# Second-half score products that run on over columns behind the keys

## The chip, the cores and the metric

The kernel runs on one core of a Trainium2 chip. The metric is the device time of one execution in microseconds (us). Several runs of each kernel are made, and their median stands for the kernel.

## What is computed

Windowed attention with four sink keys over 4 batches, 8 heads, 768 positions and 64 dimensions a head, all in float32, and behind it a two-layer block with a leaky activation, on 3072 tokens of width 512 with 2048 hidden units.

```python
scores = scale * q @ k.T                      # scale = 1/8
keep = (pos_k < n_sink) | ((pos_q - pos_k >= 0) & (pos_q - pos_k < window))   # 4, 128
a = softmax(where(keep, scores, -1e9)); x = a @ v          # heads side by side: (3072, 512)
h = x @ w_in; g = max(h, 0) + alpha * min(h, 0); out = g @ w_out
```

## The kernel before

The 3072 tokens are cut into 12 chunks of 256 queries, each of which belongs to one batch. A chunk goes through attention, and its 16 blocks of 128 hidden units then go through the two layers. While the layers of chunk c run, the attention of chunk c + 1 is mixed in between, so that TensorE always has products to do. All operations are first described to a planner (class `Plan`), each with an assumed cost, and the planner writes out one fixed order for each engine. The order depends on the assumed costs and on nothing else.

**Score products** (function `unit`, lines 569 to 601). A unit is chunk c, head h and half u: 128 queries against 260 keys (128 of the block before, 4 sink keys, 128 of the query's own block). For chunks 2 to 11 it is two products that add up in one PSUM bank: line 597 with the high part of the queries as weights, line 598 with the low part, both over the same 260 columns of keys. In the first half (u = 0) of the chunks that open a batch (3, 6 and 9) there is no block before, and the products are 132 columns wide. Chunks 0 and 1 use another form (line 588).

Keys and queries of one head lie in one SBUF tile, `kq`, side by side: 392 columns of keys (`KC`), 256 of the queries' high part, 256 of their low part (`prep_head`, line 552). The second half reads the keys from column 132 to column 392, the end of the keys, so that what lies next in the tile is the queries' high part. There are two `kq` tiles, used in turn by the heads. The halves write into banks of the kind "s", of which there are two with 512 columns each, in turn.

**What reads the scores** (`soften`, line 603). VectorE adds the mask, keeps the row's extreme and writes to SBUF (line 610); it waits for the product of line 598, and when it is through, the bank is free for a later unit. ScalarE then takes the exponential (line 614). Later `finish_head` divides by the sums and the rest of attention follows.

**The layers.** `gemm1` does 12 products of 256 columns for each block of hidden units (line 894), ScalarE and VectorE make the activation (lines 898 to 901), and `gemm2` does six products of 512 columns (lines 931, 932 and 929). All products have a weight load of their own of 128 columns, which the profile lists apart (PEld).

In TensorE's order, a second-half pair stands mostly between the 12 products of line 894 and the six of `gemm2`; a first-half pair stands between `gemm2` and the next 12.

Of the kernel before, what the change touches and what calls it, by code (L numbers as in the profile page):

```python
# [22 lines left out]
NS = 4  # L23
WIN = 2 * P + NS
# [54 lines left out]
class Plan:  # L79
# [25 lines left out]
    def op(self, engine, cost, run, reads=(), writes=(), tail=0.09, mode=None, nbytes=0, other=None, locks=False):  # L105
        o = Op(engine, cost, tail, run, self.rank if engine == "PE" else None)
        o.ways = {engine: (cost, run)}
        if other:
            o.ways[other[0]] = other[1:]
        o.born = self.rank  # L110
        if engine == "PE":
            self.rank += 1
        o.mode, o.nbytes, o.index = mode, nbytes, len(self.ops)
        seen = []
        for group, writing in ((reads, False), (writes, True)):
            for x in group:
                v, key = x if isinstance(x, tuple) else (x, None)
                if v not in seen:
                    seen.append(v)
                keys = [k for k in set(v.wrote) | set(v.read) if key is None or k is None or k == key]  # L120
                for k in keys:
                    o.before.update(v.wrote.get(k, ()))
                    if writing:
                        o.before.update(v.read.get(k, ()))
                if writing:
                    for k in keys:
                        if key is None or k == key:
                            v.wrote.pop(k, None)
                            v.read.pop(k, None)
                    v.wrote.setdefault(key, []).append(o)  # L130
                else:
                    v.read.setdefault(key, []).append(o)
        for v in seen:
            v.left += 1
        o.values = seen
        o.takes = [v for v in seen if v.kind]
        o.locks = locks
        self.ops.append(o)
        return o
# [168 lines left out]
def mm(n):  # L308
    return 0.456e-3 * n


def native(n):
    return 1.667e-3 * n
# [8 lines left out]
def program(ctx, tc, qk, pairs, vp, vq, vs, w, par, out):  # L322
    nc = tc.nc
# [245 lines left out]
    def unit(c, h, u):  # L569
        if h == 0 and u == 0:  # L570
            nms[c], sink[c], sums[c] = val("nm"), val("sink"), val("sm")
            if c in SPLIT:
                s0 = sink[c]
                op("POOL", 0.15, lambda: nc.gpsimd.memset(s0.at, 0.0), writes=[s0])
        ko = u * (P + NS)
        qs = slice(u * P, (u + 1) * P)
        w0 = slice(0 if c % CPB or u else P, WIN)
        n = w0.stop - w0.start
        kw = slice(ko + w0.start, ko + WIN)
        if c in SPLIT:  # L580
            pair = (h, h + 1)
            banks_ = [val("s") for _ in pair]
            used = [prep[c, h][0]]

            def scores():
                for x, bk in zip(pair, banks_):
                    st, r = prep[c, x]
                    nc.tensor.matmul(bk.at[:, w0], st.at[r, :QC][:, qs], st.at[r, QC:][:, kw], start=True, stop=True)
            op("PE", 1.47 * native(n), scores, reads=used, writes=banks_, tail=N_TAIL, mode="row")
        else:  # L590
            pair = (h,)
            banks_ = [val("s")]
            kq, qh, ql, ks = prep[c, h]

            def scores():
                s = banks_[0].at
                nc.tensor.matmul(s[:, w0], qh()[:, qs], ks()[:, kw], start=True, stop=False)  # L597
                nc.tensor.matmul(s[:, w0], ql()[:, qs], ks()[:, kw], start=False, stop=True)  # L598
            op("PE", 2 * mm(n), scores, reads=[kq], writes=banks_, tail=R_TAIL)
        for x, bk in zip(pair, banks_):  # L600
            soften(c, x, u, bk)

    def soften(c, h, u, s):
        if u == 0:
            ptile_[c, h] = val("pt_")
        pt, nm, sm = ptile_[c, h], nms[c], sums[c]
        i = min((c % CPB) * 2 + u, 2)
        w0 = slice(0 if i else P, WIN)
        n = WIN if i else P + NS
        op("DVE", dve(n), lambda: nc.vector.tensor_tensor_reduce(  # L610
            out=pt.at[:, u, w0], in0=s.at[:, w0], in1=masks[:, i, w0], scale=-0.125, scalar=BIG,
            op0=ALU.add, op1=ALU.min, accum_out=nm.at[:, h, u:u + 1]),
            reads=[s, known("masks"), known(f"masks{i}")], writes=[(pt, u), (nm, (h, u))], tail=0.17)
        op("ACT", exp(n), lambda: nc.scalar.activation(  # L614
            pt.at[:, u, w0], pt.at[:, u, w0], AF.Exp, bias=nm.at[:, h, u:u + 1], scale=-1.0, accum_out=sm.at[:, h, u:u + 1]),
            reads=[(nm, (h, u))], writes=[(pt, u), (sm, (h, u))])
# [331 lines left out]
    def attention(c):  # L948
        def a_step(h, u):
            def run():  # L950
                if u == 0:
                    if h == 0 and c == PAIRED:
                        masks_in_order()
                    if h == 0 and c and c % CPB == 0:
                        vs_prep(c // CPB)
                    prep_head(c, h)
                    next_load()
                unit(c, h, u)
                if u == 1:
                    finish_head(c, h)  # L960
                    first = 1 if c >= PAIRED else 5
                    if h in range(first, first + (KT if c >= PAIRED else 2)):
                        load_v(c, h - first)
            return run
# [8 lines left out]
        if c in SPLIT:  # L973
            def pair_step(h, u):
                def run():
                    if u == 0:
                        for x in (h, h + 1):
                            prep_head(c, x)
                        for x in (h, h + 1):
                            next_load()  # L980
                    unit(c, h, u)
                    if u == 1:
                        for x in (h, h + 1):
                            finish_head(c, x)
                        if h in (0, 2) and c:
                            load_v(c, h // 2)
                return run
            steps = [pair_step(h, u) for h in range(0, H, 2) for u in range(2)]
            for at, st in ((8, lambda: av_split(c, 1)), (8, lambda: sk(1)), (5, lambda: av_split(c, 0)), (4, sk)):
                steps.insert(at, st)  # L990
            return steps
# [286 lines left out]
```

## Time and profile before

| | us |
|---|---|
| median of 3 runs | 677.34 |
| lowest, highest | 676.94, 677.88 |
| span of the profiled execution | 676.2 |
| TensorE busy, products | 663.8 |
| VectorE busy | 525.8 |
| ScalarE busy | 397.5 |

The span runs from the first instruction to the last in the profiled execution; the time of a run also holds what lies around it, so that the profiled execution stands 1.1 us under the median of the runs. Products overlap one another in TensorE's pipeline, and their listed durations are longer than the distance from one to the next; what a product costs in a stream is read from the chain of waits, which gives each only the time by which it moved the end.

### The profile page before, as it was taken

Reading aid. Unit: us, or ns where it says so; the run is one execution under the profiler, and the core shown is the slowest. Engines: PE = TensorE matmul, PEld = TensorE weight load, DVE = VectorE, ACT = ScalarE, POOL = GpSimd, SP = SyncE. Lnnn points to the kernel's source line nnn. Section 1 sums busy time; section 2 is a strip of 40 time slices with the busy share of each in tenths; the row PEclk is TensorE's granted clock in tenths of the full one; section 3 lists DMA queues with packets and bytes.
Section 4 is the critical chain, followed back from the end, with each engine's and each line's share of the span. In section 5 each row is a group of like instructions: output and inputs, shape, how many; then the busy total and the mean of one; then the engine's idle time right before and its main releaser. Section 6 shows DMA issues by size and latency. Waiting matters only on the chain.

```text
span 676.2 us, 13243 instructions
## 1 busy us (share of the span) xinstructions
PE 663.8 (98%) x4532; PEld 580.5 (86%) x4534; DVE 525.8 (78%) x1750; ACT 397.5 (59%) x1066; POOL 34.5 (5%) x115
## 2 busy tenths in 40 slices
PE   9989999999999999999999999999999999999996
PEld 4577898888989989989988988988998988998995
DVE  6999999968967976986986995995895994994331
ACT  6989888827636726736636735644744753853332
POOL 2110000001000000000000000010000000000000
PEclk9979999999999999999999999999999999999999
DMA  8684641424343453443443433552542543420001
GB/s 314 229 277 151 241 187 39 127 71 147 122 133 107 122 148 93 145 132 95 141 118 114 143 107 93 163 140 61 172 128 78 161 128 88 142 94 17 32 2 35
DMA packets 58683, 85.19 MB, mean 126 GB/s; under 512 B 9072, under 2 KB 35056, under 8 KB 58608
## 3 DMA queue, kind: packets, MB, share of 16 engines
q1 hardware_dynamic: 55056, 71.17, 34.7%
q10 hardware_dynamic: 3552, 13.11, 5.4%
q8 instruction: 37, 0.61, 0.4%
q14 instruction: 38, 0.31, 0.1%
HBM read 67.22 MB, written 17.04 MB: 125 GB/s over the span
## 4 chain that ended last, share of the span: by engine, by line
PE 83%; DVE 9%; ACT 5%; issue 2%; POOL 0%; DMA 0%; ACTq 0%; SPq 0%; POOLq 0%
PE bank L894 35%; PE bank L931 12%; PE bank L932 11%; PE bank L929 11%; PE bank L786 3%; PE bank L598 3%; PE bank L597 3%; PE bank L875 2%; DVE wa L396 2%; ACT pt L614 1%; ACT wa L382 1%; DVE wa L394 1%; DVE w L404 1%; DVE g L899 1%; DVE gl L901 1%
## 5 line engine op out<-in xcount | busy, mean ns | idle before, releaser
L894 PE MATMUL bank<-xh,w 128*128 128x256 f32 x1536 | 307.9, 283 | 0.4 <-DVE g L899 0.2
L894 PEld LDWEIGHTS bank<-xh,w 128*128 128x128 f32 x1536 | 250.6, 189 | 9.0 <-DVE g L899 3.0
L894 PE MATMUL bank<-xl,w 128*128 128x256 f32 x768 | 215.1, 280 | 0.1
L898 ACT ACTIVATE g<-bank,param 128x256 f32<-128x256 f32 x192 | 90.5, 472 | 117.4 <-PE bank L894 113.1
L931 PE MATMUL bank<-w,gh 128*128 128x512 f32 x382 | 151.7, 397 | 0.2 <-ACT gh L900 0.2
L932 PE MATMUL bank<-w,gh 128*128 128x512 f32 x382 | 150.1, 393 | 0.0
L894 PEld LDWEIGHTS bank<-xl,w 128*128 128x128 f32 x768 | 145.2, 189 | 4.4 <-DVE xl L808 0.3
L614 ACT ACTIVATE pt<-pt,nm 128x260 f32<-128x260 f32 (+1 forms) x192 | 94.5, 493 | 53.5 <-DVE nm L610 53.1
L899 DVE TENSOR_TENSOR g<-bank,g 128x256 f32<-128x256 f32 x192 | 79.7, 419 | 51.4 <-ACT g L898 50.9
L929 PE MATMUL bank<-w,gl 128*128 128x512 f32 x382 | 119.5, 394 | 0.0
L900 ACT CAST gh<-g 128x256 fp32r<-128x256 f32 x192 | 76.9, 404 | 59.7 <-DVE g L899 59.6
L901 DVE TENSOR_TENSOR gl<-g,gh 128x256 fp32r<-128x256 f32 x192 | 80.5, 423 | 26.5 <-ACT gh L900 23.0
L610 DVE CUSTOM_DVE_ANT_0 pt<-bank,masks 128x260 f32<-128x260 f32 (+1 forms) x192 | 75.0, 401 | 19.3 <-PE bank L598 15.5
L929 PEld LDWEIGHTS bank<-w,gl 128*128 128x128 f32 x382 | 70.7, 188 | 16.2 <-issue 0.7
L931 PEld LDWEIGHTS bank<-w,gh 128*128 128x128 f32 x382 | 71.9, 188 | 9.5 <-ACT gh L900 0.7
L932 PEld LDWEIGHTS bank<-w,gh 128*128 128x128 f32 x382 | 71.9, 188 | 8.3
L563 DVE TENSOR_TENSOR kq<-stage,kq 64x392 fp32r<-64x392 f32 x80 | 45.3, 566 | 2.7
L659 POOL TENSOR_TENSOR sink<-pt,ri 128x8 f32<-128x8 f32 x80 | 20.8, 264 | 504.7 <-DVE ri L644 358.8
L597 PE MATMUL bank<-kq 128*128 128x260 f32 (+1 forms) x160 | 44.4, 278 | 1.3 <-DVE nm L610 1.3
L598 PE MATMUL bank<-kq 128*128 128x260 f32 (+1 forms) x160 | 45.0, 281 | 0.0
L655 DVE CUSTOM_DVE_ANT_0 comb<-pt,ri 128x128 f32<-128x128 f32 x136 | 43.1, 343 | 0.4
L561 ACT CAST kq<-stage 128x392 fp32r<-128x392 f32 x80 | 40.9, 512 | 0.7 <-ACT pt L614 0.2
(130 smaller groups left out, 686.9 us busy)
## 6 DMA issues: line engine op xcount, KB each, us to landing
stage<-qk SPq DMA_DIRECT2D x80, 324.0 KB, 2.9
wraw<-w ACTq DMA_DIRECT2D x12, 1024.0 KB, 5.9
swap<-comb SPq DMA_DIRECT2D x36, 256.0 KB, 2.0
comb<-swap SPq DMA_DIRECT2D x36, 256.0 KB, 3.2
v<-vq SPq DMA_DIRECT2D x36, 192.0 KB, 2.5
out_dram<-ob SPq DMA_DIRECT2D x22, 256.0 KB, 3.5
wraw<-w SPq DMA_DIRECT2D x4, 1024.0 KB, 12.0
v<-vp SPq DMA_DIRECT2D x8, 192.0 KB, 6.9
```

The source lines that it names most:

```text
L597: nc.tensor.matmul(s[:, w0], qh()[:, qs], ks()[:, kw], start=True, stop=False)
L598: nc.tensor.matmul(s[:, w0], ql()[:, qs], ks()[:, kw], start=False, stop=True)
L610: op("DVE", dve(n), lambda: nc.vector.tensor_tensor_reduce(out=pt.at[:, u, w0], in0=s.at[:, w0], in1=masks[:, i, w0], scale=-0.125, scalar ...
L614: op("ACT", exp(n), lambda: nc.scalar.activation(pt.at[:, u, w0], pt.at[:, u, w0], AF.Exp, bias=nm.at[:, h, u:u + 1], scale=-1.0, accum_ou ...
L894: nc.tensor.matmul(h(), fin.at[:, 0, part, ks], rhs.at[:, kt], start=(kt == 0 and n == 0), stop=(kt == KT - 1 and n == 2))
L898: op("ACT", act(QC, True), lambda: nc.scalar.activation(g.at, h(), AF.Copy, scale=alt[:, f:f + 1]), reads=[bk, known("param")], writes=[g])
L899: op("DVE", dve(QC), lambda: nc.vector.tensor_tensor(g.at, h(), g.at, ALU.max), reads=[bk], writes=[g])
L900: op("ACT", cast(QC), lambda: nc.scalar.copy(gh.at, g.at), reads=[g], writes=[gh])
L901: op("DVE", dve(QC), lambda: nc.vector.tensor_tensor(gl.at, g.at, gh.at.bitcast(F32), ALU.subtract), reads=[g, gh], writes=[gl])
L929: nc.tensor.matmul(o2[j].at, gl.at[:, js], fin.at[:, 1, 0], start=False, stop=(f == NF - 1))
L931: nc.tensor.matmul(o2[j].at, gh.at[:, js], fin.at[:, 1, 0], start=(f == 0), stop=False)
L932: nc.tensor.matmul(o2[j].at, gh.at[:, js], fin.at[:, 1, 1], start=False, stop=False)
```

## The change

In the second halves (u = 1) of chunks 2 to 11, both score products of head h read 4(h + 1) columns more, from 4 for head 0 to 32 for head 7. The columns come from the same tile, directly behind the keys, where the queries' high part lies, and the results go to the columns behind the scores in the same bank, 260 to 291 at most. Nothing reads these results. In the first halves `more` is zero, and nothing changes. The cost that the planner is told stays `2 * mm(n)` with n = 260, so the order of the instructions is the same, and their number too.

```diff
             kq, qh, ql, ks = prep[c, h]
+            more = u * NS * (h + 1)
 
             def scores():
-                s = banks_[0].at
-                nc.tensor.matmul(s[:, w0], qh()[:, qs], ks()[:, kw], start=True, stop=False)
-                nc.tensor.matmul(s[:, w0], ql()[:, qs], ks()[:, kw], start=False, stop=True)
+                s, beyond = banks_[0].at, slice(w0.start, WIN + more)
+                keys = kq.at[:, ko + w0.start:ko + WIN + more]
+                nc.tensor.matmul(s[:, beyond], qh()[:, qs], keys, start=True, stop=False)
+                nc.tensor.matmul(s[:, beyond], ql()[:, qs], keys, start=False, stop=True)
             op("PE", 2 * mm(n), scores, reads=[kq], writes=banks_, tail=R_TAIL)
```

## Rows read from the trace of the kernel before

**Rows 1.** The page: busy time by engine, and the chain that ended last by engine.

```profile
PE 663.8 (98%) x4532; PEld 580.5 (86%) x4534; DVE 525.8 (78%) x1750; ACT 397.5 (59%) x1066; POOL 34.5 (5%) x115
...
PE 83%; DVE 9%; ACT 5%; issue 2%; POOL 0%; DMA 0%; ACTq 0%; SPq 0%; POOLq 0%
```

**Rows 2.** Windows of 60 us: busy us (instructions) by engine, granted clock, DMA share, GB/s.

```profile
60.00:120.00 60.00, 59.30 (x397) 52.84 (x398) 58.70 (x113) 50.26 (x101) 1.67 (x3) 1.00 0.46 158
120.00:180.00 60.00, 58.66 (x401) 50.80 (x400) 49.97 (x193) 37.60 (x112) 4.03 (x12) 1.00 0.39 117
...
300.00:360.00 60.00, 60.00 (x433) 53.46 (x433) 44.54 (x156) 31.82 (x91) 1.94 (x8) 1.00 0.42 125
```

**Rows 3.** The chain by line in 98 to 165 us, then in 165 to 600 us.

```profile
by line: PE bank L894 25.9%; PE bank L931 8.6%; PE bank L932 8.3%; PE bank L929 7.6%; DVE wa L396 5.2%; PE bank L786 4.6%; issue 4.3%; PE bank L597 3.8%; DVE kq L563 3.6%; DVE wa L394 3.4%; PE bank L728 2.7%; DVE kq L565 2.7%; PE bank L598 
...
by line: PE bank L894 42.8%; PE bank L931 13.9%; PE bank L929 13.8%; PE bank L932 13.8%; PE bank L598 3.7%; PE bank L597 3.5%; PE bank L786 3.2%; PE bank L875 2.9%; PE bank L859 0.9%; DVE comb L655 0.2%; issue 0.2%; DVE wa L770 0.2%; DVE co
```

**Rows 4.** TensorE products by line and shape: count, busy us, mean ns, idle before, releaser.

```profile
L931 PE MATMUL bank<-w,gh 128*128 128x512 f32 x382 | 151.7, 397 | 0.2 <-ACT gh L900 0.2
L932 PE MATMUL bank<-w,gh 128*128 128x512 f32 x382 | 150.1, 393 | 0.0
L929 PE MATMUL bank<-w,gl 128*128 128x512 f32 x382 | 119.5, 394 | 0.0
L597 PE MATMUL bank<-kq 128*128 128x260 f32 x136 | 39.0, 286 | 1.3 <-DVE nm L610 1.3
L598 PE MATMUL bank<-kq 128*128 128x260 f32 x136 | 38.4, 282 | 0.0
...
L597 PE MATMUL bank<-kq 128*128 128x132 f32 x24 | 5.5, 228 | 0.1
```

**Rows 5.** The chain, 268 to 274 us: start us, us, what (both halves 260 wide).

```profile
268.54 1.36 PE bank L894 x12
269.90 0.12 PE bank L597
...
270.14 0.23 PE bank L931
...
271.53 0.12 PE bank L597
...
271.77 1.41 PE bank L894 x12
273.19 0.12 PE bank L597
```

**Rows 6.** The chain, 311 to 313.3 us: a first half 132 wide.

```profile
311.34 0.06 PE bank L597
311.40 0.11 PE bank L598
311.51 1.47 PE bank L894 x12
312.98 0.12 PE bank L597
```

**Rows 7.** Weight loads in order of time, 311.1 to 311.6 us.

```profile
311.18 0.19 PEld L598 LDWEIGHTS bank<-kq 128*128 128x128 f32 x1
311.29 0.19 PEld L894 LDWEIGHTS bank<-xh,w 128*128 128x128 f32 x1
311.40 0.19 PEld L894 LDWEIGHTS bank<-xl,w 128*128 128x128 f32 x1
```

**Rows 8.** Waits of TensorE: us in total, times, longest.

```profile
PE bank L597 <- DVE nm L610: 1.3, 3, 0.8
```

**Rows 9.** Who waits for the second score product (line 598): us, times.

```profile
  DVE pt L610: 15.5, 21
```


## The prediction

> **What bounds the kernel now.** I read the page first, for who is busy and whose work ends last, then the busy time in stretches, then the chain of waits in those stretches, and last the distances between products in the chain. TensorE is busy for 98% of the span and holds 83% of the chain [rows 1]; VectorE, at 78%, holds 9% of it. In stretches the picture has two parts. From 60 to 180 us VectorE and TensorE take turns: TensorE has gaps (59.30 and 58.66 of 60 us busy), VectorE 58.70 of 60 in the first of the two [rows 2]. From 180 to 540 us each 60 us show 60.00 us of products at a granted clock of 1.00, the upper of the two levels, 2.4 GHz; one such row stands in [rows 2], as the others read the same. The chain says it by line: from 165 to 600 us the layers' products, the scores and the weighted values make up nearly 99% of it, whereas from 98 to 165 us the visible lines of TensorE make only 61.5%, with one more cut off at the edge [rows 3]. So a product that gets longer after 165 us moves the end by what it grew; before that, by something like six tenths.
>
> **What the change adds.** For each chunk from 2 to 11 the second halves of the eight heads grow by 4, 8, ... 32 columns, together 4 x 36 = 144 columns for one product. Each pair has two products, so 288 columns a chunk, and 2880 in ten chunks, over 160 products. Nothing else is added: the instructions are as many as before, and the planner is told the old cost, so each engine's order stays as it was, with the DMA queues. Nothing is removed.
>
> **The price of a column** is not in the trace for widths between 260 and 292, so I bound it from two sides with the nearest widths. By durations: 512 columns take 397, 393 and 394 ns, mean 394.7; 260 columns take 286 and 282, mean 284 [rows 4]. That is 110.7 ns for 252 columns, 0.439 ns each. Between 132 and 260 columns on line 597 it is (286 - 228) / 128 = 0.453. The ends of products are modelled, so the distances in the chain are the better witness. Six products of 512 lie between 270.14 and 271.53 us, 1.39 / 6 = 231.7 ns each, 0.4525 ns a column; twelve of 256 take 1.36 to 1.41 us, 0.443 to 0.459 a column [rows 5]. All agree within 5%. I take 0.45, from the chain, since its widths lie on both sides of the score product, and 0.439 and 0.46 as the ends. The sum is 2880 x 0.45 = 1.30 us (1.26 to 1.32). The score pair itself fits: 269.90 to 270.14 us is 0.24 for two products, 0.12 each [rows 5], where 260 x 0.45 = 0.117.
>
> **Where it lies.** Nine chunks or nearly so have their scores where the chain is TensorE alone, so their columns count in full. Chunk 2 (its pairs run from 98 to 131 us) has a full price of 288 x 0.45 = 0.13 us, of which some 0.6 count by its share of the chain [rows 3]: 0.05 less. Of chunk 3 a part lies before 165 us, another 0.02 less. What remains is 1.23, say 1.25 us: the profiled span of 676.2 would be 677.45, and the median, which stands 1.14 above it, 677.34 + 1.25 = 678.6.
>
> **Edits with no price.** The moving operand now also reads columns of the queries' high part. The first product already reads that part as weights, and ScalarE wrote it in one instruction, for which TensorE had to wait before; no new wait. When the tile is used again, ScalarE first writes the keys, and that already waits for the pair's second product; the queries' part comes after it on the same engine. In the bank, columns 260 to 291 have no reader, and the next product into this bank waits for VectorE's read of the scores as it did. If that cover failed, each of 80 pairs would hold ScalarE for some tens of nanoseconds, which is the size of the rival on delay below. No DMA moves.
>
> **The scores arrive later.** VectorE's line 610 waits for the second product in 21 places, 15.5 us in all [rows 9]. There it starts later by the growth of both products, 2 x 0.45 x 4 to 32 = 3.6 to 28.8 ns, mean 16 ns. In the other places VectorE is behind anyway. The work after it (exponential, weighted values) has lead: TensorE waited for a bank that VectorE still held in three places only, 1.3 us in all [rows 8]. I price this at nothing; if it is paid, it is a rival.
>
> **Rival 1: a product is paced by its weight load, and the columns are free.** Behind a first half of 132 columns the weight loads follow one another at 311.18, 311.29 and 311.40 us, 0.11 us apart [rows 7], as if the load and not the columns set the pace. And the total speaks for it: the narrow pair with twelve products after it takes 311.34 to 312.98, 1.64 us [rows 6], while the wide pair with twelve takes 271.53 to 273.19, 1.66 [rows 5]; 256 columns fewer saved 0.02 us instead of 0.115. So narrowing a product under 256 columns saves nearly nothing. Would widening cost nearly nothing? Only if the load also takes the 0.12 us that the 260-wide products stand apart. The loads are at 0.11, and the 512-wide products, which cover any load, cost the same per column as the others, so a product of 260 is already on the side of the columns, if by little. If instead the load held at 0.12 and columns ran at the full 2.4 GHz, 288 columns would fit, and only head 7 would pay, 4 columns x 20 products, 0.03 us: 677.4. If half of them hide, 678.0.
> The Trainium skill, in TensorE: Matmul & The Clock Gate, section Back-to-back issue gap, speaks for a cheap column too: it gives about 81 ns for a product of 128 columns and 131 for one of 512 when loads and products alternate, so estimated from that page a column costs 50 / 384 = 0.13 ns and the change 0.37 us, 677.7. The trace disagrees at the wide end, 231.7 ns against 131 [rows 5]. The chance of this rival is 0.10.
>
> **Rival 2: the delay is paid twice, and the kernel is slower by more than its columns.** The mechanism is the hand-over from the pair's second product to line 610 and of the bank back to line 597. It decides where VectorE stands idle for line 598 and the next pair comes before the bank is free: 21 places of the first kind, 3 of the second [rows 8, 9]. If every pair were such a place, 80 x 16 ns = 1.3 us would come on top, 679.9; if a fourth to a half of them, 0.3 to 0.65 us, 678.9 to 679.25. Against it: TensorE has no gap after 180 us. Chance 0.12.
>
> **Rival 3: it doesn't do what it says, or helps.** If `more` were zero in effect, the time would stay at 677.3; the code gives 4(h + 1) for u = 1, so 0.02. A gain over 0.2% would need that a later start lets VectorE take something more urgent first; each engine's order is fixed, so 0.03 (676.0).
>
> **How the numbers follow.** A change of 0.2%, 1.35 us, is about what a measurement of this kernel can tell from none. The forecast has 0.73. It lies at 678.6 with 678.2 to 679.0 around it (the ends of the price are 0.06 wide; the runs of before lie within 0.5 us of their median), and the bound of 678.69 cuts it: 0.44 below, 0.29 above. Same: 0.44 + 0.10 (rival 1) + 0.02 = 0.56. Slower: 0.29 + 0.12 (rival 2) = 0.41. Faster 0.03. The range runs from 677.7 to 679.3: it leaves out rival 1 at its full size, a gain, no effect and the far end of rival 2, together under 0.2.
>
> **What would show it.** In the trace of the changed kernel the second-half pairs of head 7 should take 2 x 32 x 0.45 = 29 ns more in the chain than 0.24 us, those of head 0 about 4 ns; the listed durations of lines 597 and 598 should rise from about 284 ns by 0.44 to 0.45 ns a column, to 298 for head 7. The layers' products should keep their 1.36 to 1.41 and 1.39 us, and TensorE's waits stay near 1.3 us on line 597. The forecast is wrong if the pairs grow and the twelve products behind them shrink by as much (rival 1), if TensorE gets gaps at line 597 after 180 us (rival 2), or if pairs grow by more than 0.46 ns a column, which would mean that the price goes in steps or that the tile's second region costs something to read.

## The result and the profile after

| | before, us | after, us |
|---|---|---|
| median (runs) | 677.46 (20) | 678.61 (20) |
| lowest, highest | 676.47, 679.0 | 677.94, 680.88 |
| span of the profiled execution | 676.2 | 678.2 |

The ratio is 1.0019, with a 95% interval from 1.0012 to 1.0026: 1.3 us more, between 0.8 and 1.8. The forecast was 678.6.

The page of the changed kernel, busy time and chain by engine, answers to [rows 1]: TensorE's products hold 2.0 us more, and which engine bounds the kernel has not changed.

```profile
PE 665.8 (98%) x4534; PEld 582.0 (86%) x4534; DVE 526.8 (78%) x1750; ACT 398.1 (59%) x1066; POOL 34.3 (5%) x115
...
PE 83%; DVE 9%; ACT 5%; issue 2%; POOL 0%; ACTq 0%; POOLq 0%
```

Of the span's 2.0 us, 0.6 lie ahead of anything that was changed: the first score product of chunk 2 starts at 99.1 us and not at 98.5. Over all the profiles of this study that start moved between 96.9 and 99.1 us, and it goes with the granted clock of the first 60 us. That clock was 0.94 in the four profiles with a start from 98.5 on (before and after are two of them), 0.97 in the nine with a start from 97.4 to 98.0, and 1.00 in the one at 96.9. The rows of the changed kernel and of that last one, which only moves the scores in the bank (columns as in [rows 2]):

```profile
0.00:60.00 60.00, 55.63 (x333) 36.22 (x333) 51.16 (x144) 49.27 (x126) 9.65 (x32) 0.94 0.71 253
...
0.00:60.00 60.00, 54.54 (x343) 34.95 (x345) 52.70 (x148) 51.64 (x130) 9.82 (x32) 1.00 0.71 253
```

So part of the scatter of single executions goes with the clock ahead of the changed products, and profiles are compared from the first pair of chunk 2 on. (Before and after both have 0.94; the 0.6 us between them is something else, which no run here shows.) From there to the last pair of chunk 11 the changed kernel took 1.38 us longer.

One reading from before has to be put right here. The recorded runs took 1.9 to 2.1 us more than their own spans, and not 1.1: the profiled execution after, 678.2 us of span, took 680.19. So the profiled execution before, with 676.2, is one of the longer ones and not 1.1 us under a typical one. The forecast of the median doesn't suffer, as the same offset stands on both sides of the change.

In windows of 60 us TensorE is still full from 180 to 540 us, at the granted clock of 1.00, the upper level:

```profile
120.00:180.00 60.00, 58.74 (x401) 50.91 (x400) 49.90 (x194) 37.34 (x111) 4.23 (x13) 1.00 0.40 120
...
300.00:360.00 60.00, 60.00 (x437) 53.64 (x436) 45.23 (x158) 31.33 (x89) 1.93 (x8) 1.00 0.41 123
```

The pairs themselves, in order of time (start us, us, engine, line): in chunk 5, head 3 with 276 columns, a first half with 260, and further on head 7 with 292. The distance from a pair's first product to whatever comes behind is 0.26, 0.24 and 0.27 us.

```profile
270.75 0.29 PE L599 MATMUL bank<-kq 128*128 128x276 f32 x1
270.88 0.29 PE L600 MATMUL bank<-kq 128*128 128x276 f32 x1
271.01 0.39 PE L933 MATMUL bank<-w,gh 128*128 128x512 f32 x1
...
272.39 0.28 PE L599 MATMUL bank<-kq 128*128 128x260 f32 x1
272.51 0.28 PE L600 MATMUL bank<-kq 128*128 128x260 f32 x1
272.63 0.28 PE L896 MATMUL bank<-xh,w 128*128 128x256 f32 x1
```

```profile
286.66 0.29 PE L599 MATMUL bank<-kq 128*128 128x292 f32 x1
286.80 0.30 PE L600 MATMUL bank<-kq 128*128 128x292 f32 x1
286.93 0.40 PE L933 MATMUL bank<-w,gh 128*128 128x512 f32 x1
```

The mean of these distances, over the pairs after 165 us, worked out from the starts in the trace (eight or nine pairs for a widened size; the other one or two of its ten lie before). The third row sets each widened pair of chunks 3 to 11 against the same pair of the kernel before, and the last is what 0.45 ns a column would make:

| columns | 132 | 260 | 264 | 268 | 272 | 276 | 280 | 284 | 288 | 292 |
|---|---|---|---|---|---|---|---|---|---|---|
| pair, ns, after | 172 | 238.2 | 244.9 | 243.1 | 248.5 | 253.2 | 259.6 | 259.3 | 264.2 | 267.3 |
| more than the same pair before | | | 3 | 6 | 8 | 18 | 19 | 25 | 23 | 32 |
| at 0.45 ns a column | | | 4 | 7 | 11 | 14 | 18 | 22 | 25 | 29 |

Before, 117 pairs of 260 columns stood at 238.6 ns on average, most of them, by their place, at 234 to 235 or at 241. From 260 to 292 columns it is 29.1 ns for 64 columns, 0.45 ns each. The growth follows the price within 4 ns, but not evenly: heads 3 and 4 grew alike, and heads 5 and 6. All growths together make 1.19 us for 2,528 columns, 0.47 ns each. The listed durations of the second product (count, busy us, mean ns; [rows 4] has those of before) rise with them, 297 ns for head 7 against 282:

```profile
L600 PE MATMUL bank<-kq 128*128 128x260 f32 x56 | 15.8, 282 | 0.0
...
L600 PE MATMUL bank<-kq 128*128 128x292 f32 x10 | 3.0, 297 | 0.0
```

And the score products wait no longer for their bank. TensorE's waits there, and then those who wait for the second product, which answer to [rows 8] and [rows 9]; ScalarE's write of the next keys into the tile (line 561) waited once for 0.2 us, as before:

```profile
PE bank L599 <- DVE nm L612: 1.2, 3, 0.8
```

```profile
  DVE pt L612: 16.2, 22
...
  ACT kq L561: 0.2, 1
```

### The profile page after: what moved, and what is told of

Read it like the earlier page. It is cut to its first block, busy times and chain, and to the rows that moved or that the text cites. A ratio compares the mean times of both kernels' runs of the same rounds, so it can differ in the third digit from the quotient of the medians.

```text
span 678.2 us, 13245 instructions
## 1 busy us (share of the span) xinstructions
PE 665.8 (98%) x4534; PEld 582.0 (86%) x4534; DVE 526.8 (78%) x1750; ACT 398.1 (59%) x1066; POOL 34.3 (5%) x115
## 4 chain that ended last, share of the span: by engine, by line
PE 83%; DVE 9%; ACT 5%; issue 2%; POOL 0%; ACTq 0%; POOLq 0%
PE bank L896 35%; PE bank L933 11%; PE bank L931 11%; PE bank L934 11%; PE bank L788 3%; PE bank L600 3%; PE bank L599 3%; PE bank L877 2%; DVE wa L396 2%; ACT wa L382 1%; ACT pt L616 1%; DVE wa L394 1%; PE bank L1088 1%; DVE w L404 1%; DVE g L901 1%
## 5 line engine op out<-in xcount | busy, mean ns | idle before, releaser
L612 DVE CUSTOM_DVE_ANT_0 pt<-bank,masks 128x260 f32<-128x260 f32 (+1 forms) x192 | 75.1, 401 | 20.8 <-PE bank L600 16.2
L599 PE MATMUL bank<-kq 128*128 128x260 f32 (+9 forms) x160 | 45.1, 282 | 1.2 <-DVE nm L612 1.2
L600 PE MATMUL bank<-kq 128*128 128x260 f32 (+9 forms) x160 | 45.6, 285 | 0.0
```

The costliest lines, as they stand in the source:

```text
L599: nc.tensor.matmul(s[:, beyond], qh()[:, qs], keys, start=True, stop=False)
L600: nc.tensor.matmul(s[:, beyond], ql()[:, qs], keys, start=False, stop=True)
L612: op("DVE", dve(n), lambda: nc.vector.tensor_tensor_reduce(out=pt.at[:, u, w0], in0=s.at[:, w0], in1=masks[:, i, w0], scale=-0.125, scalar ...
```

## The experiments

The theory is that a column behind the keys costs what any column costs in a full stream of products, 0.45 ns, and is paid on TensorE's path. Against it stand the pace of weight loads (rival 1), the delay that is paid twice (rival 2), and a price of the place that is read. All times are set against runs of the kernel before on the same chip. In the table, "body" is the growth from the first score pair of chunk 3 to the last of chunk 11 in one profile against that of before, which leaves the scatter of the start and chunk 2 out. The last column is the part of it in the changed pairs, each against the same pair before (without the last pair of chunk 11); what is missing to the body lies in products that no edit touched.

| kernel | columns more | ratio (95%) | us more | chunk 2, us | body, us | changed pairs, us |
|---|---|---|---|---|---|---|
| the change | 2,880 | 1.0019 (1.0012 to 1.0026) | 1.3 | 0.04 | 1.33 | 1.19 |
| 32 for every head | 5,120 | 1.0037 (1.0025 to 1.0049) | 2.5 | 0.25 | 2.33 | 2.10 |
| 104 behind | 16,640 | 1.0114 (1.0092 to 1.0135) | 7.7 | 0.49 | 6.72 | 6.87 |
| 120 behind | 19,200 | 1.0134 (1.0119 to 1.0149) | 9.1 | 0.57 | 7.97 | 7.43 |
| 120 behind, moved in the bank | 19,200 | 1.0141 (1.0126 to 1.0156) | 9.6 | 0.63 | 7.87 | 7.43 |
| 120 behind, of the low part | 19,200 | 1.0123 (1.0108 to 1.0138) | 8.3 | 0.64 | 7.86 | 7.43 |
| 104 in front | 16,640 | 1.0091 (1.0069 to 1.0112) | 6.2 | 0.47 | 5.67 | 6.43 |
| 120 in front | 19,200 | 1.0099 (1.0084 to 1.0114) | 6.7 | 0.55 | 5.94 | 7.39 |
| 128 in front | 20,480 | 1.0112 (1.0092 to 1.0133) | 7.6 | 0.51 | 6.91 | 8.02 |
| scores moved in the bank | 0 | 1.0 (0.9989 to 1.0012) | 0.0 | 0.02 | 0.06 | 0.00 |
| low part cut to 132 | -10,240 | 1.001 (1.0001 to 1.002) | 0.7 | -0.24 | 0.61 | -3.90 |
| 252 in chunk 7 | 8,064 | 1.0049 (1.0036 to 1.0062) | 3.3 | 0.00 | 3.40 | 3.64 |
| 252 in chunk 2 | 8,064 | 1.0046 (1.0032 to 1.006) | 3.1 | 2.79 | -0.08 | none |

In every kernel that widens pairs behind chunk 2, these pairs grew by 0.43 to 0.47 ns for each of their columns. The rest of the body, between -1.45 and 0.54 us there, is taken up below.

### Many columns behind: price and delay

```diff
-            more = u * NS * (h + 1)
+            more = 120 * u
```

> Every second-half pair of chunks 2 to 11 runs 120 columns past the keys, whatever the head: 160 products x 120 = 19,200 columns. Columns at a fixed price of 0.45 ns on TensorE's path: 8.6 us, less 0.35 for chunk 2, whose price counts by some six tenths, so 8.3 us over the kernel before (ratio 1.012). A pace set by weight loads, with the columns hidden or partly so: 2.5 us or less if a column costs 0.13 ns; 6.2 us if the load holds 0.12 us and the columns run at the full 2.4 GHz. Delay paid twice: VectorE gets the scores 108 ns later in 80 pairs, up to 8.6 us on top, 12 to 17 us.

It took 686.34 us against 677.41, 9.1 us more (8.1 to 10.1), or 0.47 ns a column (0.42 to 0.53). That is the theory's 8.3, a little above. The cheap column (2.5 us) and the load that hides up to 0.12 us (6.2) are out, and so is the delay at its full size (12 to 17). The chain shows the price in the pair; each product moved the end by 0.17 us in place of 0.12, and the pair stands at 344.0 ns on average, 0.44 ns for each of 240 columns:

```profile
208.11 0.17 PE bank L599
208.29 0.17 PE bank L600
...
209.85 0.12 PE bank L599
209.97 0.12 PE bank L600
```

VectorE gets the scores 105 ns later in each of these pairs. It does wait for them in more places (29, 20.6 us), and ScalarE's write of the next keys in ten, 2.1 us. But the score products wait for VectorE no longer than before: 1.0 us in two places, all of it before 180 us.

```profile
PE bank L599 <- DVE nm L612: 1.0, 2, 0.7
```

### Every head 32 columns: is it paid in steps?

```diff
-            more = u * NS * (h + 1)
+            more = 32 * u
```

> Every second-half pair 32 columns wider, whatever the head: 160 x 32 = 5,120 columns. At 0.45 ns each 2.3 us, less 0.1 for chunk 2: 2.2 us (ratio 1.0033). Hidden behind weight loads: 0.2 to 0.7 us. If columns were paid in steps of 16, 260 columns would already cost 272, and 292 would cost 304: 2.3 us too, but pairs of 264 to 272 columns in the changed kernel would stand as far apart as pairs of 260.

2.5 us more (1.7 to 3.3), where 2.2 was expected. Hiding behind weight loads (0.2 to 0.7) falls. On the steps of 16 the total can't decide, but the table of pairs above does: pairs of 264 to 272 columns stand 5 to 10 ns wider than those of 260, and pairs of 292 in this kernel stand at 268.0 ns, as in the changed one. Whether there are finer steps isn't shown.

### Fewer columns: does the weight load set the pace?

The high part keeps its 260 columns, the low part reads only the last 132; the low part of the first 128 is left out of the result.

```diff
-                nc.tensor.matmul(s[:, w0], ql()[:, qs], ks()[:, kw], start=False, stop=True)
+                o = P if u else w0.start
+                nc.tensor.matmul(s[:, o:WIN], ql()[:, qs], ks()[:, ko + o:ko + WIN], start=False, stop=True)
```

> In the second halves the second product (low part of the queries) covers only the last 132 of the 260 columns; the low part of the first 128 is left out of the result. 80 products lose 128 columns each, 10,240 in all; the number of products and weight loads is unchanged. If columns alone set the price: 4.6 us less, some 4.4 with chunk 2 counted in part (ratio 0.9935). If a weight load of 0.110 to 0.115 us is the floor under a product that is now 0.12: 80 x 4 to 9 ns = 0.3 to 0.7 us less (ratio 0.999 to 0.9995).

The 10,240 columns fewer gave back nothing: 1.001 (1.0001 to 1.002), if anything slower. Columns alone (4.4 us less) are refuted in this direction. The other expectation (0.3 to 0.7 us less) isn't met by the total either, but it is at the place itself: over the body the pairs shrank by 3.90 us and the six products behind them grew by 3.56, so that 0.34 us less remain. That fits rival 1's mechanism below 260 columns. The chain shows where the saving goes:

```profile
272.12 0.12 PE bank L597
272.24 0.06 PE bank L599
272.30 0.28 PE bank L932
272.58 0.23 PE bank L933
```

The narrow product takes 0.06 us, and the first product behind it 0.28 in place of 0.23. On average the six products behind these pairs take 1.438 us in the chain against 1.385 before: 53 ns come back of the 55 by which the pair shrank. That the product behind has to wait for its weights is the likely reason. The weight loads around the pair follow one another 0.11 to 0.12 us apart, though the narrow product needs only half of that; a wait for a load as such is not shown.

```profile
271.96 0.19 PEld L599 LDWEIGHTS bank<-kq 128*128 128x128 f32 x1
272.08 0.19 PEld L932 LDWEIGHTS bank<-w,gh 128*128 128x128 f32 x1
272.19 0.19 PEld L933 LDWEIGHTS bank<-w,gh 128*128 128x128 f32 x1
```

What makes the body longer all the same is growth of the twelve products behind the first halves, which this kernel doesn't touch: 1.05 us (in the chain 1.421 us a block against 1.405). What that is, the runs in front and behind come back to.

### One chunk alone: how much of a column is paid early and late

```diff
-            more = u * NS * (h + 1)
+            more = 252 if c == 7 else 0        # the other kernel: c == 2
```

> The same 252 columns for the 8 second-half pairs of chunk 7 alone, where TensorE shows no gap and the chain is TensorE alone: 4,032 columns x 0.45 ns = 1.8 us over the kernel before (ratio 1.0027). The delay of the scores by 227 ns a pair would add up to 1.8 us more if VectorE's lateness came back to TensorE.

> Only chunk 2 is changed: its 8 second-half pairs run 252 columns past the keys, 512 columns a product, 16 x 252 = 4,032 columns, 1.81 us of TensorE at 0.45 ns. Chunk 2's scores lie from 98 to 131 us, where TensorE holds about six tenths of the chain of waits: 1.1 us over the kernel before if the share of the chain is the right discount, 1.8 if every column counts, near 0 if VectorE hides them.

These expectations count the second halves alone, but the kernels as written widened both halves of the chunk: 16 pairs, 32 products, 8,064 columns (in the first halves the first 132 of the 252 are further keys). Each of their numbers has to be doubled: 3.6 us for chunk 7, and for chunk 2 2.2 by the share of the chain, 3.6 in full. Chunk 7 took 3.3 us more (2.4 to 4.2), 0.41 ns a column. In the profile the 16 pairs grew by 3.64 us, the whole price, and 0.24 came back in products that no edit touched. Every product is 0.23 us in the chain, as one of the layers with 512 columns is:

```profile
365.96 0.23 PE bank L599
366.19 0.23 PE bank L600
366.43 1.36 PE bank L896 x12
367.79 0.23 PE bank L599
368.02 0.24 PE bank L600
```

A delay of 227 ns in 16 pairs running left no wait of TensorE at line 599 after 180 us, so nothing of rival 2 shows even at this size.

Chunk 2 took 3.1 us more (2.2 to 4.1). The interval reaches from six tenths to the whole price; the profile has 2.79 us of 3.63 between the first pair of chunk 2 and the first of chunk 3, 77%, and nothing after it. Six tenths, read off the chain's share, was too low for so large an addition. The chain by line from 98 to 165 us is in keeping with a reason: the more columns, the less of the stretch is left to VectorE. In [rows 3] the visible lines of TensorE make 61.5%; here they make 89.8%, with the pair's first product at 7.3% in place of 3.8%.

```profile
by line: PE bank L896 34.0%; PE bank L933 12.7%; PE bank L934 12.1%; PE bank L931 10.3%; PE bank L599 7.3%; PE bank L600 6.1%; PE bank L788 4.6%; PE bank L730 2.7%; DVE kq L563 2.0%; DVE pt L612 1.3%; issue 1.3%; DVE kq L565 1.3%; ACT kq L5
```

### The same columns in front of the keys

```diff
-                nc.tensor.matmul(s[:, w0], qh()[:, qs], ks()[:, kw], start=True, stop=False)
-                nc.tensor.matmul(s[:, w0], ql()[:, qs], ks()[:, kw], start=False, stop=True)
+                all_, keys = slice(w0.start, WIN + 120 * u), ks()[:, ko + w0.start - 120 * u:ko + WIN]
+                nc.tensor.matmul(s[:, all_], qh()[:, qs], keys, start=True, stop=False)
+                nc.tensor.matmul(s[:, all_], ql()[:, qs], keys, start=False, stop=True)
```

> The same 120 columns more in every second-half pair, but in front: the moving operand begins 120 columns earlier and holds keys alone, and VectorE reads the scores 120 columns further on in the bank; nothing is read from the queries' part of the tile. If a column costs the same wherever it lies: 8.3 us, as with 120 columns behind, within 0.5 us. If reading into the queries' part has a price of its own: clearly less than there.

6.7 us (5.7 to 7.7), 2.4 less than with the columns behind, which by the expectation speaks for a price of the place. 0.4 us of it lie ahead of chunk 2, and the bodies differ by 2.0. But it isn't in the pair: its products take 0.17 us each here too, and pairs stand at 343.3 ns on average against 344.0.

```profile
209.67 1.36 PE bank L896 x12
211.03 0.17 PE bank L598
211.20 0.17 PE bank L599
...
212.75 0.12 PE bank L598
212.87 0.12 PE bank L599
212.99 1.39 PE bank L896 x12
214.38 0.17 PE bank L598
```

The difference lies in products that no edit touches. The twelve of line 894 (896 here), one block of hidden units, take from 1.36 us up to 1.44 in most places, and up to 1.68 in a few. In the kernel with columns in front the blocks from 209.67 and 212.99 take 1.36 and 1.39 us. In the one with columns behind, the same two take 1.42 and 1.41:

```profile
210.09 1.42 PE bank L896 x12
...
213.25 0.12 PE bank L599
213.37 0.12 PE bank L600
213.49 1.41 PE bank L896 x12
```

Of 133 such blocks after 205 us, 61 were at most 1.40 us before, 51 with 120 columns behind and 90 with 120 in front, and their sums are 187.25, 187.68 and 186.61 us. By the starts in the trace, the 2.0 us between the bodies lie nearly all in two places: 1.38 us in the blocks directly behind a first-half pair, and 0.67 in the six products directly behind the widened pair.

Inside a block the products stand at two distances, 113 to 114 ns or 117 to 119, and a block can go over from one to the other. Of 1,565 distances after 205 us, 580 were at most 114 ns before, 454 with the columns behind and 786 with them in front.

### What about the place?

Three kernels take the two apart. The first only moves the second halves' scores to bank columns 120 to 379, with no column more:

> No more columns than in the kernel before; only the place in the bank changes: second-half scores of chunks 2 to 11 go to bank columns 120 to 379, and VectorE reads them there. If the place in the bank is what made 120 columns in front 2.4 us cheaper than 120 behind: 2.4 us less than the kernel before (ratio 0.9965). If the moving operand (which columns are read, and their values) or the timing is the cause: the same as before within 0.7 us.

The second moves the result of the kernel with 120 columns behind to bank columns 120 to 499:

> The kernel with 120 columns behind the keys in every second-half pair, with the whole result moved 120 columns on in the bank (120 to 499), where VectorE reads the scores. If the place in the bank is the cause of the difference: 6.7 us over the kernel before, as with the columns in front. If what is multiplied is the cause: 9.1 us, as with the columns behind.

The third exchanges the two query parts in the tile, so that 120 columns of the low part are read behind the keys:

> 120 columns behind the keys in every second-half pair, but the two query parts of the tile have changed places, so that the columns read are those of the queries' low part, whose values are some thousand times smaller. If the values multiplied are the cause of the difference: 6.7 us over the kernel before or less. If the place in the bank, or columns behind rather than in front, is the cause: 9.1 us. If the rest of the kernel merely falls into one rhythm or another: anywhere from 6.5 to 9.5 us, without relation to either.

The move alone gives 1.0 (0.9989 to 1.0012), the moved kernel with columns behind 1.0141 (1.0126 to 1.0156), the one that reads the low part 1.0123 (1.0108 to 1.0138). The profiles are sharper than the times: the bodies grew by 0.06, 7.87 and 7.86 us, against 7.97 with 120 columns behind. So neither the place in the bank nor the size of the values has a part in it. That left a rhythm which 120 columns in front just happened to hit:

> 128 columns of keys in front in every second-half pair, instead of 120. If columns in front are cheaper by their place, at the 0.35 ns that 120 of them cost: 160 x 128 x 0.35 = 7.2 us over the kernel before (ratio 1.0106). If the low total of 120 in front was a rhythm into which the layers' products fell with just that width, the price goes back towards 0.45 ns: 9.2 us, or anywhere between.

> 104 columns of keys in front in every second-half pair. By place, at 0.35 ns a column: 5.8 us over the kernel before (ratio 1.0086). By rhythm: not on one line with 120 and 128 in front, up to 7.5 us.

> 104 columns behind the keys in every second-half pair, instead of 120. By place, at the 0.47 ns that 120 columns behind cost: 7.8 us over the kernel before (ratio 1.0115). By rhythm: off that line by up to 2 us either way, down to 5.8.

They took 7.6 us (6.2 to 9.0), 6.2 (4.7 to 7.6) and 7.7 (6.2 to 9.1), against 7.2, 5.8 and 7.8 by place. The times alone leave room for either, as their intervals are wide. The profiles are clearer: of the 133 blocks, 90, 88 and 88 took at most 1.40 us with 120, 128 and 104 columns in front, and 51, 50, 49 and 76 with columns behind (120; 120 moved in the bank; 120 of the low part; 104). So it is not one lucky width: the three in front agree. But the width counts too, as 104 columns behind lie between. With 104, moreover, 0.44 us of the 1.05 between the bodies are in the pair itself, which stands at 336.1 ns behind and 329.7 in front.

The point in time alone is not the cause. In the kernel with chunk 2 alone widened, chunks 3 to 11 come 2.8 us later after chunk 2 began, and their products take what they took before: the body differs by 0.08 us. What in reading keys alone, or from another starting column, sets the pace of products that come later is open; no run here shows it.

## Why the prediction was right

**The bound.** It holds: from 180 to 540 us TensorE is full in every window, before and after, and a product that grows there is paid. 252 columns in chunk 7 alone cost 3.3 us of the 3.6 that their price makes, and the pairs themselves all of it.

**The price of a column.** Foretold 0.45 ns, between 0.439 and 0.46, from the distances of products with 256 and 512 columns. The pairs show 0.45 from 260 to 292 columns on average, 0.47 when each is set against itself before, and 0.44 to 380. The 0.47 lies just over the 0.46 that the prediction named as a sign of steps or of a price of the tile's second region. The excess is 0.05 us in all, and with 120 columns of the same region the price is 0.44, so it doesn't grow with what is read there; why single widths lie up to 4 ns off is open. Widths on both sides of the unseen one were the right rows to take the price from.

**The sum.** Foretold 1.30 us for all columns and 1.25 with what chunk 2 and 3 save; measured 1.3, of an interval that is 1.0 us wide. The profile agrees with 1.38 us from first pair to last: 0.04 in chunk 2, 1.19 in the pairs behind it, 0.14 in products that no edit touched. The blocks of twelve did not keep their times one by one, as the prediction had it (17 of 133 took 1.36 us before and one after), but their sum moved by 0.2 us only. That the median came out within 0.01 us of the forecast is luck, as the runs scatter by more than 0.5 us, and the other products alone moved by up to 2.0 us between kernels that differ in where they read.

**Chunk 2.** Foretold 0.08 us of its 0.13. The profiles show no fixed share: 0.04 us here, 0.25 of 0.23 with 32 columns for every head, 0.57 of 0.86 with 120, 2.79 of 3.63 with 252. The share of the chain is a fair first guess, and it is too low when the addition itself makes TensorE the later engine.

**No price for the reads behind the keys.** Right for waits: the changed kernel's score products wait for VectorE as before, ScalarE's next write of keys too, and with 120 columns pairs stand as far apart behind as in front. Not quite right for the total: with 120 columns the place made 2.0 us in the body, by the pace of other products. In the real change, all that lies outside the pairs is 0.14 us.

**Rival 1** failed as the prediction put it, and by its argument: a product of 260 columns already lies on the side of the columns. On the other side the runs fit its mechanism: 10,240 columns taken away saved nothing. The page in the Trainium skill, TensorE: Matmul & The Clock Gate, section Back-to-back issue gap, gives figures from which a column is estimated at 0.13 ns; the runs disagree: 120 columns more would be 2.5 us by it, and 9.1 were measured.

**Rival 2** did not occur: VectorE waited for the second product in 22 places and 16.2 us, against 21 and 15.5, and TensorE in three places and 1.2 us. With 120 columns TensorE's waits for that bank were still no longer.

**Rival 3**: each widened width stands in the trace, so the change does what it says; nothing became faster.

## What to carry to other kernels

Where one engine is full and its chain is unbroken, useless work on it costs its plain price, here down to a few nanoseconds a pair, and that price can be read from the distance of neighbouring products in the chain rather than from their listed durations. The price need not be symmetrical: products of 260 columns, near the spacing of weight loads, cost their columns when they were widened and gave next to nothing back when the second of each pair was narrowed, as the products behind took the time. When an addition of one microsecond is to be measured, look at where it was made in the trace: the rest of the kernel can shift by as much.

## What the runs showed of the hardware

At a granted clock of 1.00, products of one kind, with 256 columns and a weight load each, stood at two distances, 113 to 114 ns (580 of 1,565 before) or 117 to 119 (782). Which of them a block of twelve had was fixed by its position: the blocks of chunks 4 and 5 took the same times one after the other, for example 1.36 us from 209.28 and 1.41 from 212.51 in chunk 4, and 1.41 again from 265.27, its counterpart in chunk 5. In chunks 6 and 9, whose first-half pairs are 132 columns wide, the blocks behind those pairs took 1.44 to 1.47 us.

Edits to the score pairs, which come between the blocks, changed the number of blocks with at most 1.40 us from 61 of 133 to between 49 and 90, and the sum of all 133 by up to 1.1 us between kernels with the same number of columns. Neither the bank columns of the scores, nor the size of the values, nor a later start explained it.
